# Attention scores two groups ahead in the main loop of a fused attention and two-layer expert kernel

## The chip, the cores and the metric

The kernel runs on one NeuronCore of a Trainium2 chip. The metric is the device time in microseconds (us) of one execution, as the median of several runs. Beside it stands one profiled execution with its trace, from which all durations here are read. TensorE does the matmuls and the transposes of 128x128 blocks, VectorE (DVE) and ScalarE (ACT) the elementwise work, GpSimd (POOL) a few small operations and the indirect transfers, SyncE (SP) issues most transfers.

## The reference

Three parts follow each other. Attention works inside chunks of 64 positions, for 8 batches and 8 heads of width 64; a feed-forward layer squares the relu; the last part sends each of 4608 tokens to one of 8 experts. Everything is float32.

```python
# attention, per chunk of 64 of the 576 positions (9 chunks a batch)
scores = scale * np.matmul(q_c, k_c.transpose(0, 1, 2, 4, 3))
scores = scores - np.max(scores, axis=-1, keepdims=True)
attn = np.exp(scores)
attn = attn / (np.sum(attn, axis=-1, keepdims=True) + 1e-09)
out = np.matmul(attn, v_c)
# x: (4608, 512)
h = np.maximum(x @ w_in, 0.0)          # (4608, 2048)
x = (h * h @ w_out)                    # (4608, 512)
# routing: normalised x against 8 normalised expert vectors, argmax, softmax weight
# per expert e: out[mask] = gate_w[mask, None] * (np.maximum(x[mask] @ w1[e], 0.0) @ w2[e])
```

## The kernel before

The 4608 tokens are cut into 18 groups of 256 (`TG`); a group holds four chunks of 64 positions. Groups 0 and 1 run in an opening part with its own planner. The main loop, `for n in range(2, NG)`, runs groups 2 to 17, one after the other, in the order in which the code is written: each engine takes its instructions in that order, and waits for what an instruction needs.

In one pass `n` of the loop TensorE does the feed-forward layer of group n. The **first product** (`l1`, line 389) runs over 16 tiles m: 12 matmuls each into a tile `l` of PSUM. ScalarE applies relu, square and a copy to the high half of `g` (`relu`, `square`, `ghi`), VectorE makes the low half (`glo`, line 408). The **second product** (`l2`, line 413) is done for two halves of 128 tokens (tt = 0, 1), each in four pieces u = 0 to 3 of 12 matmuls. The tiles `l` of both products share a ring `mm` of four PSUM banks. The results of the second product go through the router (`route`), whose steps stand in a list `todo`; `pop` takes one per tile m from m = 2 on, and three per piece of the second product. So the copy that empties the last bank of the second product (`a0`) comes only with m = 4 of the next pass. The router has eight products with the expert vectors (line 440), a tail of small VectorE operations (lines 460 to 467), an exponential on ScalarE (line 470), and a counting step with two small matmuls (lines 476, 477) and a transfer of the rows to `x2d`.

Between these stands the attention of the next group, n+1, in steps of one function each:

- `load_qk2`: transfers of q and k on SP's queue, into two buffers of the pool `stg`. There are 16 transfers each for q and k, or 32 each where the group's four chunks lie in two batches; group 4 (chunks 16 to 19, boundary at 18) is such a group. A buffer comes free with the transpose that reads it.
- `p1t`: one VectorE transpose for q, one for k (line 208), with m = 14 and m = 15 of the first product.
- `p2p`: the scores on TensorE (line 219), in 64x64 blocks, at piece 1 of the second product.
- `p2v`, `p2e`, `p2b`: maximum and subtraction (VectorE, lines 229, 231), exponential (ScalarE, line 234), sum, reciprocal and multiplication (VectorE, lines 239 to 242).
- `p3`: turns on TensorE (line 248) and a copy by ScalarE, at piece 4.
- `p4`: the values on TensorE (line 260), again in 64x64 blocks, at piece 5, then the high half by ScalarE and the low half by VectorE (lines 268, 269) into `xT`, which the next first product reads. There is one `xT`.

The pieces are counted through both halves, so piece 4 is the first one of the half tt = 1.

Of the kernel before, what the change touches and what calls it, by code (L numbers as in the profile page):

```python
# [7 lines left out]
F32 = mybir.dt.float32  # L8
# [4 lines left out]
AF = mybir.ActivationFunctionType  # L13
ALU = mybir.AluOpType
AX = mybir.AxisListType
# [5 lines left out]
def tile_attention_moe_moe2(  # L21
# [14 lines left out]
    V, S, G, PE = nc.vector, nc.scalar, nc.gpsimd, nc.tensor  # L36
# [4 lines left out]
    TG = 256  # L41
    KD = DM // 128
    KF = DFF // 128
# [31 lines left out]
    def f32(ap):  # L75
        return ap.bitcast(F32)
# [13 lines left out]
    duo = {}  # L90
# [72 lines left out]
    raws, at = {}, {}  # L163
# [26 lines left out]
    def load_qk2(n):  # L190
        c0 = 4 * n
        for nm, src in (("q", q), ("k", k)):
            t = stg_p.tile([128, 4, 8, 32], F32, tag="stg", name=nm)
            raws[nm, n, "w"] = t
            for h in range(4):
                for g in range(4):
                    c = 0
                    while c < 4:
                        b, r = divmod(c0 + c, CPB)
                        m = min(4 - c, CPB - r)  # L200
                        nc.sync.dma_start(
                            out=t[32 * g:32 * g + 32, h, 2 * c:2 * (c + m)],
                            in_=src[b, 4 * (g // 2) + h, 64 * r:64 * (r + m), 32 * (g % 2):32 * (g % 2) + 32].rearrange("(t i) x -> i t x", i=32))
                        c += m

    def p1t(n, nm):
        o = duo["t"].tile([128, 4, TG], F32, tag="tt", name=nm + "T")
        V.transpose(out=o.rearrange("p h (t i) -> p h t i", t=8), in_=raws.pop((nm, n, "w")))
        at[nm + "2"] = o

    def p2p(n):
        qT, kT = at.pop("q2"), at.pop("k2")
        sc = at["sc2"] = at_p.tile([128, 2, 512], F32, tag="at", name="sc")
        for u in range(2):
            for h in range(4):
                for c in range(2):
                    for j in range(2):
                        t0 = 128 * u + 64 * c
                        PE.matmul(
                            out=sc[64 * c:64 * c + 64, j, u * 256 + h * 64:u * 256 + (h + 1) * 64],  # L220
                            lhsT=qT[64 * j:64 * j + 64, h, t0:t0 + 64],
                            rhs=kT[64 * j:64 * j + 64, h, t0:t0 + 64],
                            start=True, stop=True,
                        )
# [9 lines left out]
        S.activation(out=at["ss"], in_=at["ss"], func=AF.Exp, scale=0.125)  # L234

    def p2b():
        s = at["ss"]
        sm = duo["m"].tile([128, 8, 2, 1], F32, tag="sm2", name="smm")
        V.tensor_reduce(out=sm, in_=s, op=ALU.add, axis=AX.X)
        V.tensor_scalar_add(out=sm, in0=sm, scalar1=1e-9)  # L240
        V.reciprocal(out=sm, in_=sm)
        V.tensor_tensor(out=s, in0=s, in1=sm.to_broadcast([128, 8, 2, 64]), op=ALU.mult)

    def p3():
        s = at.pop("ss")
        ps = at_p.tile([128, 2, 512], F32, tag="at", name="s3")
        for g in range(8):
            PE.transpose(ps[:, g // 4, (g % 4) * 128:(g % 4 + 1) * 128], s[:, g].rearrange("p j k -> p (j k)"), ident)
        o = at["a2"] = duo["t"].tile([128, 4, TG], F32, tag="tt", name="aT")
        S.activation(out=o.rearrange("p (u a) b -> p u (a b)", u=2), in_=ps, func=AF.Copy)  # L250

    def p4(n, x):
        aT, vts = at.pop("a2").rearrange("p a (b t) -> p (a b) t", b=2), [raws.pop(("v", 2 * n + u)) for u in range(2)]
        ps = at_p.tile([128, 2, 512], F32, tag="at", name="s4")
        for u in range(2):
            for h in range(4):
                for c in range(2):
                    for j in range(2):
                        o = u * 256 + (h // 2) * 128 + 64 * c
                        PE.matmul(  # L260
                            out=ps[64 * (h % 2):64 * (h % 2) + 64, j, o:o + 64],
                            lhsT=vts[u][64 * j:64 * j + 64, c, h, :],
                            rhs=aT[64 * j:64 * j + 64, 4 * u + h, 64 * c:64 * c + 64],
                            start=True, stop=True,
                        )
        pv = ps.rearrange("p j (w y) -> p j w y", w=2)
        hi, lo = [y.rearrange("p w (j u) t -> p j w (u t)", j=2) for y in x]
        S.activation(out=hi, in_=pv, func=AF.Copy)
        V.tensor_tensor(out=lo, in0=pv, in1=f32(hi), op=ALU.subtract)
# [111 lines left out]
    x0 = xT[:, 0], xT[:, 1]  # L381
# [16 lines left out]
    def relu(ps):  # L398
        S.activation(out=ps, in_=ps, func=AF.Relu)  # L399

    def square(ps):
        S.activation(out=ps, in_=ps, func=AF.Square)  # L402

    def ghi(ps, g):
        S.activation(out=g[:, 0], in_=ps, func=AF.Copy)  # L405

    def glo(ps, g):
        V.tensor_tensor(out=g[:, 1], in0=ps, in1=f32(g[:, 0]), op=ALU.subtract)  # L408
# [217 lines left out]
    with tc.manual_schedule():  # L626
# [19 lines left out]
        for m in range(KF):  # L646
            if m < 14:
                sl = 9 + m // 2
                t = wb[:, m % 2, sl * DM:(sl + 1) * DM].rearrange("p (a t) -> p a t", a=2)
            else:  # L650
                t = gx_p.tile([128, 2, TG], F32R, name=f"gx{m}")
# [157 lines left out]
        p = 0  # L809
# [31 lines left out]
        for r in range(4):  # L841
            nc.sync.dma_start(
                out=x2d[NT - TG:NT, :].rearrange("(p r) (a c) -> p (r a) c", r=2, a=2)[:, r], in_=zr)
# [9 lines left out]
        for n in range(2, NG):  # L853
            last = n == NG - 1
            if last:
                attn.close()
                two = ctx.enter_context(tc.tile_pool(name="two", bufs=1, reuse_waits="tile"))
                XN, XE = (ctx.enter_context(tc.tile_pool(name=nm, bufs=2, reuse_waits="tile")) for nm in ("XN", "XE"))
                p2["X"] = XN, XE
                idx = p2["idx"] = two.tile([128, E, NCOL], I32, name="idx")  # L860
                pre = ExitStack()
                stx["p"] = pre.enter_context(tc.tile_pool(name="stx", bufs=2, reuse_waits="tile"))
            gs = []
            for m in range(KF):
                g = g_p.tile([128, 2, TG], F32R, tag="g", name="g")
                gs.append(g)
                if m == KF - 2 and n == 2:
                    solo.close()
                    duo["t"] = attn.enter_context(tc.tile_pool(name="tt", bufs=2))
                    duo["s"] = attn.enter_context(tc.tile_pool(name="s2", bufs=1))  # L870
                    duo["m"] = attn.enter_context(tc.tile_pool(name="m2", bufs=1))
                if m >= KF - 2 and not last:
                    p1t(n + 1, "qk"[m - KF + 2])
                ps = l1(m, x0)
                relu(ps)
                square(ps)
                ghi(ps, g)
                glo(ps, g)
                if m == 0 and not last:
                    load_qk2(n + 1)  # L880
                if m == 0 and last:
                    for _ in range(8):
                        e_load(stg_p, "stg")
                if last and m >= 6 and m % 2 == 0:
                    e_split(stg_p, "stg", G)
                if m >= 2:
                    pop(2 if last and m < 5 else 1)
            nxt = {}
            if not last:
                load_v(2 * n + 2)  # L890
                load_v(2 * n + 3)
                nxt = {1: [lambda: p2p(n + 1), p2v, p2e], 2: [p2b], 4: [p3], 5: [lambda: p4(n + 1, x0)]}
            for tt in range(2):
                ps = mm_p.tile([128, 512], F32, tag="mm", name="l2")
                for u in range(4):
                    for fn in nxt.get(4 * tt + u, []):
                        fn()
                    l2(gs, tt, 4 * u, 4 * u + 4, ps, wo, KF)
                    if last and tt == 1 and u == 2:
                        turn(early, xT, gx[0])  # L900
                    pop((3, 3, 3, 3, 2, 1, 1, 1)[4 * tt + u] if last else 3)
                    if last:
                        for _ in range((3, 3, 2, 2, 1, 0, 0, 0)[4 * tt + u]):
                            e_split(stg_p, "stg")
                r = route(2 * n + tt, ps, xt_x if last else None)
                if last and tt:
                    r.pop(0)()
                    todo.insert(0, r.pop(0))
                todo += r
# [166 lines left out]
```

## Time and profile before

| what | value |
|---|---|
| median of 3 runs | 1432.27 us (1432.26 to 1433.1) |
| the profiled execution | 1430.2 us, its span 1428.4 us |
| TensorE busy | 1367.7 us, 96% of the span |
| VectorE, ScalarE, GpSimd busy | 791.1, 644.3, 175.2 us |
| TensorE's granted clock, mean over the span | 0.982 of full speed |
| main loop in the span | from about 150 to about 950 us |

The span reaches from the first to the last instruction that the profiler saw; the time of the execution has a little more around it. A wait is told for an engine by what it waited for: "PE sc L219 <- DVE kT L208" is TensorE, which stood before the scores until VectorE's transpose of k was done. Matmuls are pipelined and their ends are modelled, so the time that one block takes is best read from the start of the block to the start of the next one. One `PE.matmul` on float32 blocks of 64x64 shows as two instructions in the trace: a block of 32 shows as 64.

### The profile page before, as it was taken

Reading aid. Unit: us, or ns where it says so; the run is one execution under the profiler, and the core shown is the slowest. Engines: PE = TensorE matmul, PEld = TensorE weight load, DVE = VectorE, ACT = ScalarE, POOL = GpSimd, SP = SyncE. Lnnn points to the kernel's source line nnn. Section 1 sums busy time; section 2 is a strip of 40 time slices with the busy share of each in tenths; the row PEclk is TensorE's granted clock in tenths of the full one; section 3 lists DMA queues with packets and bytes.
Section 4 is the critical chain, followed back from the end, with each engine's and each line's share of the span. In section 5 each row is a group of like instructions: output and inputs, shape, how many; then the busy total and the mean of one; then the engine's idle time right before and its main releaser. Section 6 shows DMA issues by size and latency. Waiting matters only on the chain. (4 is left out here: it accounts for less than half of the span.)

```text
span 1428.4 us, 27983 instructions
## 1 busy us (share of the span) xinstructions
PE 1367.7 (96%) x10780; PEld 1221.6 (86%) x10780; DVE 791.1 (55%) x2146; ACT 644.3 (45%) x1529; POOL 175.2 (12%) x189
## 2 busy tenths in 40 slices
PE   5699999999999999999999999998999999899998
PEld 4697889988998898899889988987889898788886
DVE  6878566657656675666576556754442222145424
ACT  4693535634553554355345535633442222145424
POOL 0000010000000100000100001323212121113110
PEclk6899999999999999999999999999999999999999
DMA  8533332122122212212212222136533111156412
GB/s 212 158 119 119 104 70 57 37 38 61 39 45 38 53 39 45 45 40 44 50 35 54 43 38 90 46 119 200 181 126 99 34 60 35 43 165 199 150 49 92
DMA packets 222794, 116.81 MB, mean 82 GB/s; under 512 B 191585, under 2 KB 192227, under 8 KB 222468
## 3 DMA queue, kind: packets, MB, share of 16 engines
q1 hardware_dynamic: 213508, 89.01, 23.9%
q0 software_dynamic: 9056, 25.35, 5.6%
q8 instruction: 99, 1.62, 0.5%
q14 instruction: 99, 0.81, 0.2%
q10 hardware_dynamic: 32, 0.02, 0.0%
HBM read 94.64 MB, written 20.19 MB: 80 GB/s over the span
## 5 line engine op out<-in xcount | busy, mean ns | idle before, releaser
L389 PE MATMUL l<-xT,wa 128*128 128x256 f32 x3168 | 382.6, 281 | 6.0 <-DVE wa L157 6.0
L389 PEld LDWEIGHTS l<-xT,wa 128*128 128x128 f32 x3168 | 378.1, 189 | 8.3 <-DVE wa L157 6.7
L413 PE MATMUL l<-wb,g 128*128 128x512 f32 x1536 | 373.2, 398 | 0.0
L413 PEld LDWEIGHTS l<-wb,g 128*128 128x128 f32 x1536 | 284.0, 188 | 65.7
L440 DVE CUSTOM_DVE_ANT_0 junk<-X,en 128x512 bf16<-128x512 f32 x240 | 166.3, 693 | 64.0 <-ACT X L433 60.8
L408 DVE TENSOR_TENSOR g<-l,g 128x256 fp32r<-128x256 f32 x264 | 110.3, 419 | 160.4 <-ACT g L405 157.1
L598 DVE SCALAR_TENSOR_TENSOR h<-m,h 128x256 fp32r<-128x256 f32 x144 | 60.9, 423 | 195.6 <-ACT h L597 189.0
L413 PE MATMUL m<-wa,h 128*128 128x512 f32 x576 | 139.3, 397 | 0.0
L399 ACT ACTIVATE l<-l 128x256 f32<-128x256 f32 x272 | 100.8, 371 | 68.6 <-PE l L389 60.7
L413 PEld LDWEIGHTS m<-wa,h 128*128 128x128 f32 x576 | 106.4, 188 | 24.2
L597 ACT ACTIVATE h<-m 128x256 fp32r<-128x256 f32 x144 | 55.1, 383 | 132.8 <-PE m L594 118.0
L405 ACT ACTIVATE g<-l 128x256 fp32r<-128x256 f32 x264 | 101.5, 384 | 8.5
L402 ACT ACTIVATE l<-l 128x256 f32<-128x256 f32 x272 | 100.1, 368 | 8.7
L490 POOL DMA_INDIRECT perm<-tid,pos x36 | 38.2, 1060 | 523.2 <-DVE pos L489 281.3
L594 PEld LDWEIGHTS m<-xc,wa 128*128 128x128 f32 x768 | 92.5, 189 | 0.6
L594 PE MATMUL m<-xc,wa 128*128 128x256 f32 x768 | 92.8, 281 | 0.0
L413 PE MATMUL m<-wb,h 128*128 128x512 f32 x336 | 81.9, 398 | 0.0
L609 POOL DMA_INDIRECT out_dram<-o,idx x38 | 38.5, 1014 | 326.9 <-ACT xc L79 140.1
L413 PEld LDWEIGHTS m<-wb,h 128*128 128x128 f32 x336 | 62.0, 188 | 14.1
L608 ACT ACTIVATE o<-m,gn 128x512 f32<-128x512 f32 x23 | 15.8, 688 | 114.6 <-PE m L413 71.2
L435 POOL TENSOR_TENSOR ss<-ss,half 128x1 f32<-128x1 f32 x36 | 28.1, 780 | 308.7 <-ACT l L434 165.2
L80 DVE TENSOR_TENSOR xc<-tp,xc 128x512 fp32r<-128x512 f32 x36 | 24.3, 684 | 69.1 <-ACT xc L79 69.1
(182 smaller groups left out, 1540.2 us busy)
## 6 DMA issues: line engine op xcount, KB each, us to landing
we<-in_moe_w_dram SPq DMA_DIRECT2D x124, 256.0 KB
v<-in_v_dram SPq DMA_DIRECT2D x144, 64.0 KB
x2d<-X SPq DMA_DIRECT2D x32, 258.0 KB
ws<-in_moe_w_in_dram SPq DMA_DIRECT2D x8, 1024.0 KB
ws<-in_moe_w_out_dram SPq DMA_DIRECT2D x8, 1024.0 KB
q<-in_q_dram SPq DMA_DIRECT2D x160, 32.0 KB
k<-in_k_dram SPq DMA_DIRECT2D x160, 32.0 KB
en<-embn SPq DMA_DIRECT2D x1, 2048.0 KB
```

What stands on the lines that cost most here:

```text
L389: PE.matmul(out=ps, lhsT=wi[:, a, m // 4, kt, (m % 4) * 128:(m % 4 + 1) * 128], rhs=x[b][:, :, kt, :], start=(n == 0), stop=(n == 3 * KD - 1),
L399: S.activation(out=ps, in_=ps, func=AF.Relu)
L402: S.activation(out=ps, in_=ps, func=AF.Square)
L405: S.activation(out=g[:, 0], in_=ps, func=AF.Copy)
L408: V.tensor_tensor(out=g[:, 1], in0=ps, in1=f32(g[:, 0]), op=ALU.subtract)
L413: PE.matmul(out=ps, lhsT=gs[kk][:, b, tt * 128:(tt + 1) * 128], rhs=wt[:, a, kk, :], start=(kk == 0 and n == 0), stop=(kk == last - 1 and ...
L440: V.tensor_tensor_reduce(out=junk.rearrange("p (g c) -> p g c", g=4), in0=rows(X)[:, :, 0:128], in1=en[:, e].rearrange("p (g c) -> p g c", ...
L490: G.indirect_dma_start(out=perm[:, :], out_offset=bass.IndirectOffsetOnAxis(ap=pos[:, 0:1], axis=0), in_=tid[:, i:i + 1], in_offset=None,)
L594: PE.matmul(out=ps, lhsT=v1[:, a, m // 4, kt, (m % 4) * 128:(m % 4 + 1) * 128], rhs=xt[:, b, :, kt, :], start=(n == 0), stop=(n == 3 * KD ...
L597: S.activation(out=g[:, 0], in_=ps, func=AF.Relu)
L598: V.scalar_tensor_tensor(out=g[:, 1], in0=ps, scalar=0.0, in1=f32(g[:, 0]), op0=ALU.max, op1=ALU.subtract)
L609: G.indirect_dma_start(out=out[:, :], out_offset=bass.IndirectOffsetOnAxis(ap=col, axis=0), in_=o, in_offset=None, bounds_check=NT - 1, oo ...
```

## The change

The scores are now made two groups ahead: in pass n those of group n+2 stand directly behind the values of group n+1 (piece 5), as one block. The softmax of these scores is spread: maximum, subtraction and exponential behind them, sum and reciprocal at m = 1 of the next pass, multiplication at m = 3 (`p2m`), turns at piece 1. The loads and the transposes of q and k are for group n+2 accordingly. The turned values go back into the buffer `s`, no longer into one of the pool `tt`. Pass 2 is the way in: it does the scores of group 3 at piece 0, and loads, transposes (pieces 2 and 3) and scores (piece 6) of group 4 too.

```diff
     def p2b():
-        s = at["ss"]
-        sm = duo["m"].tile([128, 8, 2, 1], F32, tag="sm2", name="smm")
-        V.tensor_reduce(out=sm, in_=s, op=ALU.add, axis=AX.X)
+        sm = at["sm2"] = duo["m"].tile([128, 8, 2, 1], F32, tag="sm2", name="smm")
+        V.tensor_reduce(out=sm, in_=at["ss"], op=ALU.add, axis=AX.X)
         V.tensor_scalar_add(out=sm, in0=sm, scalar1=1e-9)
         V.reciprocal(out=sm, in_=sm)
-        V.tensor_tensor(out=s, in0=s, in1=sm.to_broadcast([128, 8, 2, 64]), op=ALU.mult)
+
+    def p2m():
+        s = at["ss"]
+        V.tensor_tensor(out=s, in0=s, in1=at.pop("sm2").to_broadcast([128, 8, 2, 64]), op=ALU.mult)
...
-        o = at["a2"] = duo["t"].tile([128, 4, TG], F32, tag="tt", name="aT")
-        S.activation(out=o.rearrange("p (u a) b -> p u (a b)", u=2), in_=ps, func=AF.Copy)
-
-    def p4(n, x):
+        S.activation(out=s.rearrange("p (u a) j k -> p u (a j k)", u=2), in_=ps, func=AF.Copy)
+
+    def p4(n, x=None):
...
+        at["s4"] = ps
+        if x:
+            p4x(x)
+
+    def p4x(x):
+        pv = at.pop("s4").rearrange("p j (w y) -> p j w y", w=2)
...
-                if m >= KF - 2 and not last:
-                    p1t(n + 1, "qk"[m - KF + 2])
+                if m == 1 and n > 2 and not last:
+                    p2b()
+                if m == 3 and n > 2 and not last:
+                    p2m()
+                if m >= KF - 2 and n + 2 < NG or m >= KF - 2 and n == 2:
+                    p1t(n + 1 + (n > 2), "qk"[m - KF + 2])
...
-                if m == 0 and not last:
+                if m == 0 and n == 2:
                     load_qk2(n + 1)
+                if m == 0 and 2 < n < NG - 2:
+                    load_qk2(n + 2)
...
-                nxt = {1: [lambda: p2p(n + 1), p2v, p2e], 2: [p2b], 4: [p3], 5: [lambda: p4(n + 1, x0)]}
+                join = [lambda: p4(n + 1, x0)]
+                if n + 2 < NG:
+                    join = [lambda: p4(n + 1), lambda: p2p(n + 2), lambda: p4x(x0), p2v, p2e]
+                nxt = {1: [p3], 5: join}
+                if n == 2:
+                    load_qk2(n + 2)
+                    nxt = {0: [lambda: p2p(n + 1), p2v, p2e], 2: [p2b, p2m, lambda: p1t(n + 2, "q")], 3: [lambda: p1t(n + 2, "k")], 4: [p3], 6: join}
```

In what follows, `sc<-kT,qT` are scores, `s_...<-ident,s` turns, `s_...<-aT,v` or `s_...<-s,v` values, `l_...<-xT,wa` tiles of the first product, `l_...<-wb,g` matmuls of the second.

**TensorE, pass 2**, from the last tile of the first product to the first tile of pass 3, before:

```order
203 L389 MATMUL l_2134<-xT,wa 128x256 x12
204 L413 MATMUL l_2161<-wb,g 128x512 x12
205 L219 MATMUL sc<-kT,qT 64x64 x32
206 L413 MATMUL l_2161<-wb,g 128x512 x36
207 L248 MATMUL s_2254<-ident,s 128x128 x8
208 L413 MATMUL l_2253<-wb,g 128x512 x12
209 L260 MATMUL s_2285<-aT,v 64x64 x32
210 L413 MATMUL l_2253<-wb,g 128x512 x36
211 L389 MATMUL l_2378<-xT,wa 128x256 x12
```

and with the change:

```order
203 L395 MATMUL l_2134<-xT,wa 128x256 x12
204 L219 MATMUL sc<-kT,qT 64x64 x32
205 L419 MATMUL l_2227<-wb,g 128x512 x48
206 L250 MATMUL s_2324<-ident,s 128x128 x8
207 L419 MATMUL l_2323<-wb,g 128x512 x24
208 L261 MATMUL s_2369<-s,v 64x64 x32
209 L219 MATMUL sc<-kT,qT 64x64 x32
210 L419 MATMUL l_2323<-wb,g 128x512 x24
211 L395 MATMUL l_2485<-xT,wa 128x256 x12
```

The scores of group 3 (row 205 before, 204 now) have moved ahead of the whole second product, and those of group 4 (row 209 now) have come in behind the values, ahead of the last 24 matmuls.

**VectorE, pass 2**, behind the multiplication that ends the softmax of group 3 (`junk,lg` is a router product, two rows each; `xT<-` the low half of the values), before:

```order
264 L242 TENSOR_TENSOR s<-s,smm 128x1024
265 L440 ISA junk,lg<-X,en 128x512
...
269 L269 TENSOR_TENSOR xT<-s_2285,xT 128x2x2x256
```

and with the change:

```order
264 L244 TENSOR_TENSOR s<-s,smm 128x1024
265 L208 STREAM_TRANSPOSE qT<-q 128x1024
266 L208 STREAM_TRANSPOSE kT<-k 128x1024
267 L446 ISA junk,lg<-X,en 128x512
...
277 L275 TENSOR_TENSOR xT<-s_2369,xT 128x2x2x256
278 L229 TENSOR_REDUCE mx<-sc 128x16
279 L231 TENSOR_TENSOR s<-sc,mx 128x2x8x64
280 L446 ISA junk,lg<-X,en 128x512
```

The two transposes of group 4 now stand here, ahead of all eight router products (five of them in rows 267 to 276) and of the low half of the values, and the softmax of group 4 begins behind that.

**TensorE, a regular pass** (pass 3), from the first piece of the second product, before:

```order
231 L413 MATMUL l_2793<-wb,g 128x512 x12
...
235 L477 MATMUL pr<-oh,ones 128x8
236 L219 MATMUL sc<-kT,qT 64x64 x32
237 L413 MATMUL l_2793<-wb,g 128x512 x36
238 L248 MATMUL s_2905<-ident,s 128x128 x8
239 L413 MATMUL l_2904<-wb,g 128x512 x12
240 L260 MATMUL s_2936<-aT,v 64x64 x32
241 L413 MATMUL l_2904<-wb,g 128x512 x36
```

and with the change:

```order
231 L419 MATMUL l_2873<-wb,g 128x512 x12
...
235 L483 MATMUL pr<-oh,ones 128x8
236 L250 MATMUL s_2905<-ident,s 128x128 x8
237 L419 MATMUL l_2873<-wb,g 128x512 x36
238 L419 MATMUL l_2951<-wb,g 128x512 x12
239 L261 MATMUL s_2972<-s,v 64x64 x32
240 L219 MATMUL sc<-kT,qT 64x64 x32
241 L419 MATMUL l_2951<-wb,g 128x512 x36
```

The scores have left the place behind the first 12 matmuls, where the turns stand now, and follow the values without a full-array matmul between the two. On SP's queue the 64 transfers of group 4's q and k stand where they stood, directly behind the eight of v at the end of pass 2's first product; those of group 5 now follow them directly, ahead of a transfer to `x2d`, the loads of v and another transfer to `x2d`.

## Rows read from the trace of the kernel before

**Rows 1.** The page: busy time, share of the span and instructions of TensorE, and its granted clock in 40 equal slices of the span, in tenths of full speed (9 is 90% or more).

```profile
PE 1367.7 (96%) x10780; PEld 1221.6 (86%) x10780; DVE 791.1 (55%) x2146; ACT 644.3 (45%) x1529; POOL 175.2 (12%) x189
...
PEclk6899999999999999999999999999999999999999
```

**Rows 2.** The view of waits, TensorE, from 186 to 880 us: who waited for whom, us in total, times, longest.

```profile
PE sc L219 <- DVE kT L208: 6.2, 15, 1.0
```

**Rows 3.** The timeline of TensorE in a regular pass, 430 to 464 us: start, duration, engine, line, operation, out<-in, shape, count, and in brackets the idle time before it. Durations of TensorE hold a modelled end.

```profile
434.84 1.16 PE L219 MATMUL sc<-kT,qT 64*64 64x64 f32 x64 [0.36 <-DVE kT L208]
435.93 8.66 PE L413 MATMUL l<-wb,g 128*128 128x512 f32 x36
...
445.23 3.05 PE L413 MATMUL l<-wb,g 128*128 128x512 f32 x12
448.20 1.21 PE L260 MATMUL s<-aT,v 64*64 64x64 f32 x64
449.34 8.66 PE L413 MATMUL l<-wb,g 128*128 128x512 f32 x36
457.85 5.76 PE L389 MATMUL l<-xT,wa 128*128 128x256 f32 x48
...
463.52 0.72 PE L389 MATMUL l<-xT,wa 128*128 128x256 f32 x4
```

**Rows 4.** The timeline of TensorE in two short windows at the end of the scores' and of the values' block (435.7 to 436.0 and 449.1 to 449.4 us): the last 22 of the 64 instructions of each, so the start is that of the 43rd.

```profile
435.48 0.52 PE L219 MATMUL sc<-kT,qT 64*64 64x64 f32 x22
...
448.89 0.52 PE L260 MATMUL s<-aT,v 64*64 64x64 f32 x22
```

**Rows 5.** The timeline of VectorE in the same pass, 425 to 460 us.

```profile
433.56 1.22 DVE L208 STREAM_TRANSPOSE kT<-k 128x1024 f32<-128x1024 f32 x1
...
436.44 1.22 DVE L229 TENSOR_REDUCE mx<-sc 128x16 f32<-128x1024 f32 x1
437.69 1.22 DVE L231 TENSOR_TENSOR s<-sc,mx 128x1024 f32<-128x1024 f32 x1
440.04 1.22 DVE L239 TENSOR_REDUCE smm<-s 128x16 f32<-128x1024 f32 x1 [1.13 <-ACT s L234]
...
441.80 1.22 DVE L242 TENSOR_TENSOR s<-s,smm 128x1024 f32<-128x1024 f32 x1
...
450.52 1.22 DVE L269 TENSOR_TENSOR xT<-s,xT 128x1024 fp32r<-128x1024 f32 x1 [2.04 <-ACT xT L268]
451.66 0.68 DVE L440 CUSTOM_DVE_ANT_0 junk<-X,en 128x512 bf16<-128x512 f32 x1
...
455.94 0.15 DVE L460 TENSOR_SCALAR ss<-ss 128x1 f32<-128x1 f32 x1
...
457.39 0.22 DVE L467 TENSOR_SCALAR ex<-lg,m 128x8 f32<-128x8 f32 x1
```

**Rows 6.** The timelines of ScalarE and of VectorE, 457 to 475 us, at the start of the next pass: the router's exponential, the first relu (line 399) and the first low half of `g`.

```profile
457.65 0.21 ACT L470 ACTIVATE ex<-ex 128x8 f32<-128x8 f32 x1 [7.16 <-DVE ex L467]
457.76 0.18 ACT L470 ACTIVATION_READ_ACCUMULATOR ex<-ex 128x1 f32 x1
459.45 0.37 ACT L399 ACTIVATE l<-l 128x256 f32<-128x256 f32 x1 [1.50 <-PE l L389]
...
460.67 0.42 DVE L408 TENSOR_TENSOR g<-l,g 128x256 fp32r<-128x256 f32 x1 [3.05 <-ACT g L405]
```

**Rows 7.** The timeline of TensorE in pass 2, 183 to 215 us.

```profile
185.94 2.95 PE L413 MATMUL l<-wb,g 128*128 128x512 f32 x12
189.85 1.16 PE L219 MATMUL sc<-kT,qT 64*64 64x64 f32 x64 [0.96 <-DVE kT L208]
190.95 8.66 PE L413 MATMUL l<-wb,g 128*128 128x512 f32 x36
199.44 1.04 PE L248 MATMUL s<-ident,s 128*128 128x128 f32 x8
200.23 3.04 PE L413 MATMUL l<-wb,g 128*128 128x512 f32 x12
...
212.84 2.38 PE L389 MATMUL l<-xT,wa 128*128 128x256 f32 x19
```

**Rows 8.** The timeline of SP's queue, 185 to 245 us: the issuing of transfers, with the time that SP spent on them.

```profile
191.49 16.65 SPq L201 DMA_DIRECT2D q<-in_q_dram  x32
208.24 15.89 SPq L201 DMA_DIRECT2D k<-in_k_dram  x32
224.24 0.36 SPq L480 DMA_DIRECT2D x2d<-X  x1
```

**Rows 9.** The view by windows over the k half of that load: window, its length, busy time and count of TensorE, its weight loads, VectorE, ScalarE and GpSimd, then the granted clock, the mean busy share of the 16 DMA engines, and GB/s.

```profile
208.30:224.10 15.80, 15.80 (x119) 14.86 (x118) 7.66 (x35) 8.50 (x25) 1.60 (x2) 1.00 0.22 35
```

**Rows 10.** The timeline of VectorE in pass 2, 188 to 203 us: the transpose of k of group 3.

```profile
188.48 1.23 DVE L208 STREAM_TRANSPOSE kT<-k 128x1024 f32<-128x1024 f32 x1
```

**Rows 11.** TensorE beside its longest stand in the last part of the kernel: the timeline, 1240 to 1256 us, and two windows of 4 us behind that stand, with columns as in rows 9.

```profile
1246.06 10.18 PE L594 MATMUL m<-xT,wb 128*128 128x256 f32 x68 [5.25 <-issue]
...
1246.10:1250.10 4.00, 4.00 (x19) 4.00 (x20) 0.52 (x2) 0.90 (x2) 0.99 (x1) 0.50 0.04 10
1250.50:1254.50 4.00, 4.00 (x36) 4.00 (x35) 2.53 (x6) 2.33 (x6) 2.96 (x3) 1.00 0.74 218
```

**Rows 12.** The view of transfers, 223 to 227 us: what the DMA engines moved, in GB/s, in 40 slices of 0.1 us.

```profile
GB/s 54 12 0 54 76 35 3 5 74 71 17 0 12 69 72 12 0 31 76 50 25 334 392 372 351 413 330 351 83 0 0 13 36 46 102 143 138 72 126 159
```

More of the change, by code (lines that the diff above doesn't have):

```diff
@@ L236, in p2b @@
     def p2b():
-        s = at["ss"]
-        sm = duo["m"].tile([128, 8, 2, 1], F32, tag="sm2", name="smm")
-        V.tensor_reduce(out=sm, in_=s, op=ALU.add, axis=AX.X)
+        sm = at["sm2"] = duo["m"].tile([128, 8, 2, 1], F32, tag="sm2", name="smm")
+        V.tensor_reduce(out=sm, in_=at["ss"], op=ALU.add, axis=AX.X)
         V.tensor_scalar_add(out=sm, in0=sm, scalar1=1e-9)
         V.reciprocal(out=sm, in_=sm)
-        V.tensor_tensor(out=s, in0=s, in1=sm.to_broadcast([128, 8, 2, 64]), op=ALU.mult)
+    def p2m():
+        s = at["ss"]
+        V.tensor_tensor(out=s, in0=s, in1=at.pop("sm2").to_broadcast([128, 8, 2, 64]), op=ALU.mult)
     def p3():
-        s = at.pop("ss")
+        s = at["ss"]
         ps = at_p.tile([128, 2, 512], F32, tag="at", name="s3")
@@ L248, in p3 @@
             PE.transpose(ps[:, g // 4, (g % 4) * 128:(g % 4 + 1) * 128], s[:, g].rearrange("p j k -> p (j k)"), ident)
-        o = at["a2"] = duo["t"].tile([128, 4, TG], F32, tag="tt", name="aT")
-        S.activation(out=o.rearrange("p (u a) b -> p u (a b)", u=2), in_=ps, func=AF.Copy)
-    def p4(n, x):
-        aT, vts = at.pop("a2").rearrange("p a (b t) -> p (a b) t", b=2), [raws.pop(("v", 2 * n + u)) for u in range(2)]
+        S.activation(out=s.rearrange("p (u a) j k -> p u (a j k)", u=2), in_=ps, func=AF.Copy)
+    def p4(n, x=None):
+        aT, vts = at.pop("ss").rearrange("p g j k -> p g (j k)"), [raws.pop(("v", 2 * n + u)) for u in range(2)]
         ps = at_p.tile([128, 2, 512], F32, tag="at", name="s4")
@@ L265, in p4 @@
                         )
-        pv = ps.rearrange("p j (w y) -> p j w y", w=2)
+        at["s4"] = ps
[3 more added lines that the diff above has]
+        pv = at.pop("s4").rearrange("p j (w y) -> p j w y", w=2)
         hi, lo = [y.rearrange("p w (j u) t -> p j w (u t)", j=2) for y in x]
```

## The prediction

> **What bounds the kernel now.** I read the page first: TensorE is busy for 96% of the span and its clock is at the full level from the third slice of forty on [rows 1]. So time is won only where TensorE stands still, and lost wherever it is made to. The view of waits for the stretch with the single-group loop (groups 2 to 16 prepare attention) has one entry for TensorE: the scores wait for `kT`, 6.2 us in 15 times [rows 2]. The longest, 0.96 us, is in group 2 [rows 7]; the other fourteen are 5.24 us together, 0.374 us each. In a regular group the reader sees why [rows 3, 5]: `kT` starts on VectorE at 433.56, ends at 434.78, and the scores start at 434.84, one piece of the second product after the first product's end.
>
> The rows show a second, smaller loss, at each change between the full array and the 64x64 blocks. A run of 36 matmuls of the second product takes 8.51 us up to the next start, 0.236 each [rows 3]; the 12 ahead of the values take 448.20 - 445.23 = 2.97 instead of 2.84: 0.13 to enter. Inside the blocks the step is (448.89 - 448.20)/42 = 16.4 ns for the values and (435.48 - 434.84)/42 = 15.2 for the scores [rows 4], so 64 of them are 1.05 and 0.98; the starts behind them come 1.14 and 1.09 after the block's: about 0.10 to leave. A round trip costs 0.23.
>
> **The regular groups.** Scores for group n+2 stand behind the values of n+1. Their `qT`, `kT` come at the same place of the first product as before, now some 14 us ahead of use, so the wait goes. The values leave the array in 64x64 shape, which I take as a seam of no cost: that round trip goes as well (bounds: 0 or 0.23 saved). In groups 3 to 15 each saves 0.374 + 0.23 = 0.60, thirteen times 7.85. Group 16 has no scores left: 0.374 + 0.13 + 1.09 = 1.6. Together 9.4 us.
>
> The moved work needs cover. ScalarE does the same count of operations; the turned values go back into `s`, so no `tt` buffer is needed. VectorE gets maximum and subtraction (2.5 us, from 436.44 to 438.9) behind the low half of the values, and sum with reciprocal (1.76, 440.04 to 441.80) and multiplication (1.22) inside the first product [rows 5]. From a start S of the values: the low half runs from S+2.32 to 3.54; maximum and subtraction to 6.05; six router products of 4.28 (451.66 to 455.94) to 10.33; the router's tail of 1.67 (to 457.61) to 12.0 [rows 5]. The first product starts at S + 1.05 + 0.98 + 0.10 + 8.51 = 10.64, and its first relu is 1.60 later, 12.24 [rows 3, 6]; the router's exponential ahead of it on ScalarE ends 0.33 behind the tail, 12.33. So the relu is 0.1 late. The low half of its tile starts 1.22 after the relu and takes 0.42 [rows 6]: 13.97. Sum and reciprocal reach 15.73, the next low half 16.15. Until the fifth tile the second product's last tile still holds one of the four banks, so tile m+3 takes the bank of tile m, and the fifth tile, due at 10.64 + 5.67 = 16.31, needs that second low half. It fits by 0.16. Regular groups have cover, though little.
>
> **Group 2, where the two-ahead order starts.** Here lies the largest term. Before, SP issues the loads of q and k of group 4 from 191.49 to 224.13: 64 transfers, 32.6 us, 0.51 each [rows 8]; nothing needs them until the end of group 3's first product. In the new order SP has them at the same place, behind the values' loads, and their buffers come free at the same transposes as before, so they are issued at the same times. But now both transposes of group 4 stand on VectorE in the second product of group 2, and the scores of group 4 stand on TensorE ahead of its last 24 matmuls. The last packets of k land at about 225.1: after that the view of transfers jumps to over 330 GB/s, the packets of the X row block that SP issues next [rows 12]. I take `kT` from 225.2 to 226.4 and the scores from 226.5.
>
> When does TensorE arrive? Its first product ends at 185.94. It then waits for `kT` of group 3, ready at 189.71, until 189.85, as before, but without the 12 matmuls (2.84) that ran under that wait [rows 7, 10]. Scores to 190.95; 48 matmuls, 11.33, to 202.3; turns 0.79; 24 matmuls and the entry, 5.80, to 208.9; values 1.05 to 209.9. It stands for 16.6 us. Then scores, leaving and 24 matmuls, 6.75: the next first product could start at 233.25 instead of 212.84, a loss of 20.4.
>
> VectorE waits in `kT` too, and everything behind that instruction is late: five router products (3.6), the low half of the values (1.25), maximum and subtraction (2.5), three router products (2.15), the tail (1.67). That is 11.2 us from 226.4, 237.6. ScalarE's relu follows at 237.9, the low half ends 1.22 + 0.42 later at 239.55, and the fourth tile can start at 239.6. Sum and reciprocal reach 241.3, the second low half 241.75, the fifth tile starts at 241.8. Before it would be 212.84 + 5.67 = 218.5. Loss 23.3.
>
> The clock comes on top or under this. Where TensorE stood for 5.25 us near the end, the granted clock showed the lower level (1.2 GHz), and for 4 us after work came back: 19 matmuls in 4.0 us at 0.50 against 36 at 1.00 [rows 11]. That is 4.0 x (1 - 19/36) = 1.9 us. With it the first three tiles end about 239.3, before the fourth may start at 239.6: hidden under VectorE's late chain. I add nothing.
>
> **Sum.** +23.3 - 9.4 = +13.9. The profiled execution, 1430.2 us (span 1428.4), becomes 1444.1; the median of the runs is 2.1 above the profiled one, so 1446.1 us.
>
> Bounds. Low: all 64 issues at the k half's 0.497 (15.89/32) land 0.8 earlier, and neither backlog nor lower clock shows: 20.4 - 0.8 - 9.4 = +10.2, 1442.5. High: backlog and clock added, 25.2; no round trips saved, 6.4: +18.8, 1451.1.
>
> **Rivals.**
> A: regular groups lose their cover. If the second low half comes over 0.16 us late in each group, TensorE waits for a bank in thirteen groups. Price: 0.3 more is 3.9 us, all of the saving 7.85: 1450 to 1454. For it: the margin is 0.16 on a chain of twelve durations. Against: before, VectorE idles 3.05 us ahead of that first low half [rows 6], and the moved work is counted into all of it. Chance 0.12.
>
> B, the other side: faster, because the loads land in time. SP's issue, not the data, paces them: over the k half the 16 DMA engines are 22% busy and move 35 GB/s [rows 9]. Were the data the limit, 32.6 x 0.22 is 7 us, landing near 200, `kT` near 202.5, and TensorE arrives at 209.9 without a stall. Group 2 would then cost 209.9 + 6.75 - 212.84 = 3.8, the change would give 3.8 - 9.4 = -5.6: 1426.7 us. It decides where the stall is below 5.6 us: loads landed by 214, 0.35 us an issue instead of 0.51. Against it: the same 64 transfers, from the same start, in this very trace. Chance 0.06.
> The Trainium skill (DMA: Bandwidth & Descriptors, section "Issuing engines are not separate DMA queues") says that the time in which a sequencer initiates a DMA is usually small beside the DMA itself. By that rule B would hold and the sum be its 1426.7; the trace disagrees, 32.6 us of issue against some 7 us of engine work, and the measurement decides.
>
> C: the stall comes but is shorter (another overlap, the loads started sooner): 1429 to 1441. Nothing in the trace gives it; 0.04.
>
> **How the numbers follow.** The likeliest case, the stall with regular savings, has 0.78 and gives 1446.1, with its own range 1442.5 to 1451.1. The range for all, 1441 to 1452, takes in half of A and leaves out B, C and the rest of A, some 0.16. A measurement of this kernel can tell about 0.2%, 2.9 us: faster is B, 0.06; same takes part of C, 0.03; slower 0.91.
>
> **What would show it.** Right: one wait of TensorE for `kT`, about 16.6 us, near 210 us, and one of some 3.9 near 186; no other wait for `kT`; a granted clock below 1.00 near 225 to 231; the values and scores as one block of 128 instructions from group 3 on, with 0.6 us less from one block to the next; group 3's first product about 22 us late. Wrong: `kT` of group 4 long done when TensorE gets to its scores, or waits for the tiles `l` in each regular group.

## The result and the profile after

The kernel with the change takes 1442.44 us (median of 4 runs, 1440.46 to 1444.56) against 1432.26 before (4 runs, 1431.85 to 1433.1): a ratio of 1.0071, 95% interval 1.0053 to 1.0088. It is slower, by 10.2 us, and the interval leaves out 1. The profiled execution took 1440.46 us, its span 1438.3, so 9.9 more than the span before.

The page after, lines as in [rows 1]:

```profile
PE 1367.1 (95%) x10780; PEld 1222.3 (85%) x10780; DVE 785.1 (55%) x2146; ACT 645.6 (45%) x1529; POOL 174.0 (12%) x189
...
PEclk6899997999999999999999999999999999999999
```

TensorE has the same number of instructions and, within 0.6 us, the same busy time as before. What is new is one slice, the seventh (215.7 to 251.7 us), in which the granted clock is below nine tenths. The view of waits, TensorE, 150 to 960 us, which answers to [rows 2]:

```profile
PE sc L219 <- DVE kT L208: 18.7, 2, 15.0
```

Fifteen short waits for `kT` became two long ones, both in pass 2. TensorE there, columns as in [rows 7]:

```profile
188.45 1.29 PE L219 MATMUL sc<-kT,qT 64*64 64x64 f32 x64 [3.75 <-DVE kT L208]
189.67 12.85 PE L419 MATMUL l<-wb,g 128*128 128x512 f32 x48
202.36 1.03 PE L250 MATMUL s<-ident,s 128*128 128x128 f32 x8
203.15 5.84 PE L419 MATMUL l<-wb,g 128*128 128x512 f32 x24
208.91 1.21 PE L261 MATMUL s<-s,v 64*64 64x64 f32 x64
225.12 1.99 PE L219 MATMUL sc<-kT,qT 64*64 64x64 f32 x64 [15.00 <-DVE kT L208]
227.04 7.32 PE L419 MATMUL l<-wb,g 128*128 128x512 f32 x24
234.20 5.76 PE L395 MATMUL l<-xT,wa 128*128 128x256 f32 x48
239.86 3.41 PE L395 MATMUL l<-xT,wa 128*128 128x256 f32 x27
```

Pass 3 begins at 234.20 instead of 212.84. Two stands are seen, and behind each of them blocks that are longer than usual: 48 matmuls from 189.67 to 202.36 (12.69 us; 48 of them in a regular pass take 11.38, from 453.28 to 464.66 below), scores of 1.92 us from 225.12 to 227.04 instead of 1.09, and 24 matmuls of 7.16 from 227.04 to 234.20, where the same 24 took 5.76 from 203.15 to 208.91. What the second stand waits for is on SP's queue, columns as in [rows 8], and on VectorE:

```profile
190.09 15.78 SPq L201 DMA_DIRECT2D q<-in_q_dram  x32
205.97 16.45 SPq L201 DMA_DIRECT2D k<-in_k_dram  x32
```

```profile
207.18 1.25 DVE L208 STREAM_TRANSPOSE qT<-q 128x1024 f32<-128x1024 f32 x1 [10.81 <-DMA q<-in_q_dram]
223.73 1.25 DVE L208 STREAM_TRANSPOSE kT<-k 128x1024 f32<-128x1024 f32 x1 [15.30 <-DMA k<-in_k_dram]
...
239.12 0.36 DVE L414 TENSOR_TENSOR g<-l,g 128x256 fp32r<-128x256 f32 x1
```

SP issues the 64 transfers of q and k from 190.09 to 222.42 (205.97 + 16.45), back to back, 0.505 us each. VectorE stands in each of the two transposes until its half has landed. The windows of TensorE's clock, columns as in [rows 9]:

```profile
189.30:192.70 3.40, 3.40 (x30) 2.70 (x20) 2.45 (x2) 0.40 (x1) 0.00 (x0) 0.51 0.35 73
...
225.10:230.30 5.20, 5.18 (x72) 4.41 (x73) 5.06 (x12) 0.00 (x0) 0.00 (x0) 0.50 0.37 59
230.30:235.00 4.70, 4.70 (x25) 3.94 (x24) 4.46 (x14) 1.06 (x1) 0.00 (x0) 1.00 0.40 65
```

The lower level (1.2 GHz) shows behind both stands (the times in which TensorE waits): behind the one of 3.75 us until 192.7, behind the one of 15.00 us until 230.3.

A regular pass after, beside [rows 3]; the last row is where pass 16 starts, for the mean over the passes:

```profile
427.02 5.76 PE L395 MATMUL l<-xT,wa 128*128 128x256 f32 x48
...
449.58 2.96 PE L419 MATMUL l<-wb,g 128*128 128x512 f32 x12
...
453.28 11.45 PE L419 MATMUL l<-wb,g 128*128 128x512 f32 x48
464.66 1.15 PE L261 MATMUL s<-s,v 64*64 64x64 f32 x62
...
465.70 1.10 PE L219 MATMUL sc<-kT,qT 64*64 64x64 f32 x62
466.73 8.66 PE L419 MATMUL l<-wb,g 128*128 128x512 f32 x36
475.23 0.98 PE L395 MATMUL l<-xT,wa 128*128 128x256 f32 x7
...
860.88 1.33 PE L395 MATMUL l<-xT,wa 128*128 128x256 f32 x10
```

and from the trace before, to compare with:

```profile
261.77 5.76 PE L389 MATMUL l<-xT,wa 128*128 128x256 f32 x48
...
284.34 2.03 PE L413 MATMUL l<-wb,g 128*128 128x512 f32 x8
...
408.75 5.76 PE L389 MATMUL l<-xT,wa 128*128 128x256 f32 x48
...
431.47 2.96 PE L413 MATMUL l<-wb,g 128*128 128x512 f32 x12
...
849.81 1.45 PE L389 MATMUL l<-xT,wa 128*128 128x256 f32 x11
```

Values and scores are one block (464.66 to 466.73, 2.07 us for 128 instructions; the last values and the first scores alternate). Thirteen passes, 3 to 15, take 860.88 - 234.20 = 626.68, 48.21 each; before, 849.81 - 212.84 [rows 7] = 636.97, 49.00 each. So the change does save in every regular pass what it was costed for, and more, and loses it all, and 10 us beside, in pass 2.

### The profile page after: what moved, and what is told of

Read it like the earlier page. It is cut to its first block, busy times and chain, and to the rows that moved or that the text cites. A ratio compares the mean times of both kernels' runs of the same rounds, so it can differ in the third digit from the quotient of the medians.

```text
span 1438.3 us, 28001 instructions
## 1 busy us (share of the span) xinstructions
PE 1367.1 (95%) x10780; PEld 1222.3 (85%) x10780; DVE 785.1 (55%) x2146; ACT 645.6 (45%) x1529; POOL 174.0 (12%) x189
## 5 line engine op out<-in xcount | busy, mean ns | idle before, releaser
L439 ACT ACTIVATE X<-l 128x512 f32<-128x512 f32 x32 | 19.1, 595 | 103.4 <-PE l L419 88.6
```

## The experiments

The theory: the loss is the load of group 4, 64 issues on one queue, which the way in of pass 2 needs some 15 us before they have landed; the regular passes gain. The rivals: pass 2 costs this whatever group it loads; the data, not the issue, is late; the gain in the regular passes is the wait alone.

**The way in one pass later.** In the kernel with the change, pass 2 works as before, and pass 3 is the way in; its pass needs group 5, with 32 transfers instead of 64, in place of group 4.

```diff
...
-                if m >= KF - 2 and n + 2 < NG or m >= KF - 2 and n == 2:
-                    p1t(n + 1 + (n > 2), "qk"[m - KF + 2])
+                if m >= KF - 2 and n + 2 < NG:
+                    p1t(n + 1 + (n > 3), "qk"[m - KF + 2])
...
-                if m == 0 and n == 2:
+                if m == 0 and n <= 3:
                     load_qk2(n + 1)
-                if m == 0 and 2 < n < NG - 2:
+                if m == 0 and 3 < n < NG - 2:
                     load_qk2(n + 2)
...
                 if n == 2:
+                    nxt = {1: [lambda: p2p(n + 1), p2v, p2e], 2: [p2b, p2m], 4: [p3], 5: [lambda: p4(n + 1, x0)]}
+                if n == 3:
                     load_qk2(n + 2)
```

> The changed kernel with the two-ahead order begun one pass later: pass 2 as in the kernel before, pass 3 is the way in and loads group 5 (16 transfers each for q and k instead of 32). Theory (the stall is SP's issue of group 4's 64 transfers, and it is the whole loss): kT of group 5 is ready near 256 us, before TensorE arrives near 259, so no long wait; pass 3 costs about 3.8 us more than before, twelve regular passes give 0.79 each and pass 16 gives 1.8: about 1425 us. Rival (the way in stalls wherever it stands, because both transposes lie ahead of the router on VectorE): a wait of 10 us or more in pass 3, about 1436 to 1442 us.

It took 1426.51 us (1424.07 to 1428.6), ratio to before 0.9955 (0.9938 to 0.9972). The long wait is gone. One stand is left, the first one of the way in, ahead of the scores at piece 0; pass 3 here:

```profile
211.59 5.76 PE L395 MATMUL l<-xT,wa 128*128 128x256 f32 x48
...
237.63 1.99 PE L219 MATMUL sc<-kT,qT 64*64 64x64 f32 x64 [3.33 <-DVE kT L208]
239.55 5.02 PE L419 MATMUL l<-wb,g 128*128 128x512 f32 x12
244.41 0.18 PE L482 MATMUL pr<-oh,tri 128*128 128x8 bf16 x1
...
267.27 5.76 PE L395 MATMUL l<-xT,wa 128*128 128x256 f32 x48
```

The way in by itself does not cost the 22.8 us; with the 64 transfers of group 4 it does. One term was expected too small: the way-in pass took 55.68 us (211.59 to 267.27), 6.75 over the 48.93 of the same pass before, where 3.8 were expected. The scores there stand 3.33 us, the clock is at the lower level from 237.0 to 243.8, and scores and 12 matmuls take 1.92 and 4.86 (239.55 to 244.41) instead of 1.09 and 2.80: 2.9 us that a stand of 3.33 costs beside itself.

**Half the issues.** The kernel with the change, but group 4 reads the q and k of group 5, whose chunks lie in one batch: the same bytes in 32 transfers instead of 64.

```diff
-        c0 = 4 * n
+        c0 = 4 * (5 if n == 4 else n)
```

> The changed kernel, except that group 4 takes q and k from the addresses of group 5: the same bytes in the same runs of 128 B, but 16 transfers each instead of 32 (so the q and k of group 4 are another group's, and its part of the output is changed). Theory (the number of transfers that SP issues sets the time): the load takes 16.6 us instead of 32.6, kT of group 4 is ready near 209, the wait of 15.0 us falls under 1 us, no lower clock, about 1424 us. Rival (bytes or packets set it): the load still ends near 223, the wait stays at 15 us, 1442 us.

1426.11 us (1424.8 to 1428.13), ratio 0.9953 (0.9937 to 0.997). SP's queue, VectorE, and TensorE's waits for `kT`:

```profile
190.96 8.31 SPq L201 DMA_DIRECT2D q<-in_q_dram  x16
199.37 7.79 SPq L201 DMA_DIRECT2D k<-in_k_dram  x16
```

```profile
208.76 1.25 DVE L208 STREAM_TRANSPOSE kT<-k 128x1024 f32<-128x1024 f32 x1 [6.85 <-DMA q<-in_q_dram]
```

```profile
PE sc L219 <- DVE kT L208: 3.8, 1, 3.8
```

An issue takes 0.52 and 0.49 us, though it carries twice the bytes. Half the issues end at 207.16, the transpose is done at 210.0, before TensorE has ended the values (211.5), and the 15-us stand is gone, with everything else in place: here a transfer of half the size cost the queue as much as a whole one, and the number of issues decided. The 3.8 left is the first stand, ahead of group 3's scores, with its lower clock (187.5 to 194.3), which the expectation of 1424 did not count.

**The issues shared by two engines.** The kernel with the change, the 32 transfers of k of group 4 on GpSimd.

```diff
-                        nc.sync.dma_start(
+                        (G if n == 4 and nm == "k" else nc.sync).dma_start(
```

> The changed kernel with the 32 transfers of k of group 4 issued on GpSimd's queue instead of SP's, beside those of q. Theory (issue time on one sequencer is what is short): q lands near 207; if GpSimd issues one in 0.5 us k lands there too and the wait falls under 1 us, about 1424 us; if it takes about 1 us for each, as its indirect transfers do (1.06 us), k lands near 223 and the wait stays, about 1442 us. Rival (the DMA engines are short): with both at once each is slower, the wait stays near 15 us although GpSimd has issued all by 207.

1428.67 us (1426.91 to 1431.37, 9 runs), ratio 0.9976 (0.9966 to 0.9986). GpSimd, VectorE and TensorE:

```profile
189.91 16.42 POOL L201 DMA_DIRECT2D k<-in_k_dram  x29 [2.16 <-DVE g L414]
206.76 1.71 POOL L201 DMA_DIRECT2D k<-in_k_dram  x3 [0.43 <-issue]
```

```profile
211.53 1.25 DVE L208 STREAM_TRANSPOSE kT<-k 128x1024 f32<-128x1024 f32 x1 [1.85 <-DMA k<-in_k_dram]
```

```profile
212.92 1.16 PE L219 MATMUL sc<-kT,qT 64*64 64x64 f32 x64 [1.87 <-DVE kT L208]
...
225.42 1.67 PE L395 MATMUL l<-xT,wa 128*128 128x256 f32 x12 [1.34 <-DVE g L414]
```

The same 64 transfers, issued side by side, moved 69 GB/s from 191.0 to 207.6 instead of 35, and the stand fell from 15.00 to 1.87 us. So the DMA engines had room, and one sequencer's issuing was short. The second row of TensorE is the wait for the low half of a tile, VectorE's late chain, that I had put into pass 2: it shows here, 1.34 us, where TensorE itself was less late. The time is 4.7 us over the 1424 that was expected for an issue of 0.5 us: one took 0.57 on GpSimd, k was used only at 211.53, and the first stand is here too, 3.71 us, with the lower level behind it.

**The transposes alone.** The kernel before, with the two transposes two tiles earlier from pass 3 on, and nothing else.

```diff
-                if m >= KF - 2 and not last:
-                    p1t(n + 1, "qk"[m - KF + 2])
+                lead = 2 if n == 2 else 4
+                if KF - lead <= m < KF - lead + 2 and not last:
+                    p1t(n + 1, "qk"[m - KF + lead])
```

> The kernel before, with the transposes of q and k two tiles earlier (m = 12 and 13 instead of 14 and 15) from pass 3 on. Scores stay where they were. Theory (the wait for kT is 0.374 us in each of 14 passes, and the rest of the saving of 0.79 a pass belongs to the change between full array and 64x64 blocks): the 14 waits go, 5.2 us, about 1427 us, passes of about 48.6 us. Rival (the wait is most of the saving): passes fall to about 48.2 us, about 1421 us.

1424.62 us (1424.07 to 1425.7), ratio 0.9948 (0.9932 to 0.9965). The waits and a regular pass:

```profile
PE sc L219 <- DVE kT L208: 1.0, 1, 1.0
```

```profile
477.07 2.96 PE L413 MATMUL l<-wb,g 128*128 128x512 f32 x12
...
480.01 1.16 PE L219 MATMUL sc<-kT,qT 64*64 64x64 f32 x64
...
503.00 1.22 PE L389 MATMUL l<-xT,wa 128*128 128x256 f32 x9
```

This splits the gain of a regular pass. From the first 12 matmuls of the second product to the next first product it is 26.38 us before (431.47, above, to 457.85 [rows 3]), 25.93 here (477.07 to 503.00), 25.65 with the change (449.58 to 475.23). The wait was worth 0.45, the round trip 0.28.

**Both, and the way in later.** The first of these experiments, with the transposes two tiles earlier in every pass behind pass 2, and in pass 3 the scores of group 4 back at piece 1 and the transpose of k at piece 5.

```diff
-                if m >= KF - 2 and n + 2 < NG:
-                    p1t(n + 1 + (n > 3), "qk"[m - KF + 2])
+                lead = 2 if n == 2 else 4
+                if KF - lead <= m < KF - lead + 2 and n + 2 < NG:
+                    p1t(n + 1 + (n > 3), "qk"[m - KF + lead])
...
                 if n == 3:
                     load_qk2(n + 2)
-                    nxt = {0: [lambda: p2p(n + 1), p2v, p2e], 2: [p2b, p2m, lambda: p1t(n + 2, "q")], 3: [lambda: p1t(n + 2, "k")], 4: [p3], 6: join}
+                    nxt = {1: [lambda: p2p(n + 1), p2v, p2e], 2: [p2b, p2m, lambda: p1t(n + 2, "q")], 4: [p3], 5: [lambda: p1t(n + 2, "k")], 6: join}
```

> Way in at pass 3 as in the run that began one pass later, but scores of group 4 at piece 1 and their transposes two tiles earlier, and the transpose of k of group 5 behind two router products (piece 5). Theory (the 6.7 us that pass 3 cost more there are 3.3 us of standing, 2.9 us of the lower clock behind it and the scores' block): no stand, no lower clock, pass 3 of about 49.7 us, regular passes 48.21: about 1420 to 1421 us, 3 to 4 us under the kernel with only the earlier transposes. Rival (the way in costs 5 us or more by its order alone): pass 3 of 54 us or more, about 1425 us.

1422.29 us (1419.38 to 1425.4), ratio 0.9929 (0.9915 to 0.9943). Pass 3 took 49.57, as expected, the regular passes 48.21. Pass 4 took 52.16, which was not: the other group with 64 transfers, group 6, is loaded there (issued from 250.45 to 282.97), and the earlier transposes ask for it before it can be used:

```profile
286.36 1.25 DVE L208 STREAM_TRANSPOSE kT<-k 128x1024 f32<-128x1024 f32 x1 [3.07 <-issue]
```

```profile
289.43 0.18 PE L482 MATMUL pr<-oh,tri 128*128 128x8 bf16 x1 [2.04 <-DVE oh L472]
```

VectorE stands 3.07 us in `kT`, the counting step behind it is late, and TensorE waits 2.04 us for that. The clock is at the lower level from 289.5 to 292.9. From the last issue of k to the transpose 3.39 us passed here (282.97 to 286.36), where it was 1.31 in the changed kernel (222.42 to 223.73).

**The scores away from the values.** As the last, but in the passes from 4 on the scores stand one piece (12 matmuls) behind the values, so that each has a round trip of its own.

```diff
+                if n > 3 and n + 2 < NG:
+                    nxt = {1: [p3], 5: [lambda: p4(n + 1, x0)], 6: [lambda: p2p(n + 2), p2v, p2e]}
```

> The same kernel, except that in the regular passes the scores stand at piece 6, 12 matmuls of the second product behind the values, so that the array changes to 64x64 blocks and back twice again; no wait for kT in either. Theory (one round trip costs 0.28 us of the pass): passes of 48.49 instead of 48.21 us, twelve of them 3.4 us: about 1424 us. Rival (blocks side by side save nothing, the gain is in the wait and in VectorE's order): passes stay at 48.21 us, same time as the kernel with both.

1427.02 us (1422.45 to 1430.21, 7 runs), ratio 0.9963 (0.9949 to 0.9978), 4.7 us over the kernel with both, and the intervals do not meet. A regular pass:

```profile
479.38 2.96 PE L419 MATMUL l<-wb,g 128*128 128x512 f32 x12
...
494.46 1.21 PE L261 MATMUL s<-s,v 64*64 64x64 f32 x64
495.60 3.06 PE L419 MATMUL l<-wb,g 128*128 128x512 f32 x12
498.58 1.16 PE L219 MATMUL sc<-kT,qT 64*64 64x64 f32 x64
...
505.38 5.76 PE L395 MATMUL l<-xT,wa 128*128 128x256 f32 x48
```

From 479.38 to 505.38 are 26.00 us against 25.65: the second round trip costs 0.35. The pass is longer by 0.51, not 0.28 as expected; the remaining 0.16 lies in the first product, which takes 22.71 us here (456.67 to 479.38) and 22.56 with the change (427.02 to 449.58).

Up to the end of pass 4's first product this kernel is the one with both, and its SP issued the transfers of group 6 within 0.3 us of the same times (250.14 to 282.80). Yet the transpose of k stood for 0.92 us only:

```profile
284.24 1.25 DVE L208 STREAM_TRANSPOSE kT<-k 128x1024 f32<-128x1024 f32 x1 [0.92 <-DMA k<-in_k_dram]
```

TensorE had no wait there, the clock stayed at the upper level, and pass 4 took 48.69. So the early place leaves the pass open to a late load, but the loss does not come in every execution.

**The transposes alone, again,** beside the last two on their chip.

> The kernel before with only the transposes two tiles earlier, run again beside the other two for a comparison on one chip: passes of 48.49 us, about 1424.6 us; the kernel with both is 3 to 4 us below it by the theory, level with it or above by the rival.

1423.33 us (1421.48 to 1425.78, 6 runs), ratio 0.9943 (0.993 to 0.9956), passes of 48.49 as the first time. The full two-ahead order (1422.29) is 1.0 us ahead of this one move, and the intervals overlap.

**Both, with the early transposes in pass 3 alone.**

```diff
-                lead = 2 if n == 2 else 4
+                lead = 4 if n == 3 else 2
```

> The kernel with both, with the early transposes in pass 3 alone; from pass 4 on they stand at m = 14 and 15 again, as in the changed kernel. Theory (the 52.16 us of pass 4 came from the transpose of k of group 6, whose 64 transfers SP ends only near 285, and from the lower clock behind that stand): pass 4 of 48.2 to 48.5 us, the rest as it was, some 3.7 us less: about 1418 to 1419 us. Rival (pass 4 pays for VectorE's late chain out of pass 3): pass 4 stays near 52 us, 1422 us.

1422.39 us (1419.61 to 1423.19), ratio 0.9935 (0.9921 to 0.9949). Pass 4 fell from 52.16 to 48.38, with no stand in the transposes: the later place avoids the loss, and VectorE's late chain out of pass 3 was not its cause. But with the early place too pass 4 took only 48.69 in the run above. What made k 2 us later in the one execution is open. The time of 1418 to 1419 that was expected was nearly met by the profiled execution (1419.61), not by the median. The profiled execution of the version before it was its longest run (1425.4): whether group 6 was late in its other runs is not known, and by their times the two versions can't be told apart.

## Why the prediction was right, and where its sizes were off

The forecast was 1446.1 us and slower; the median is 1442.44, inside the range of 1441 to 1452, near its lower end, and 0.06 below the likeliest case's own range (1442.5). The terms, span against span:

| stretch | predicted | measured | from |
|---|---|---|---|
| opening part | 0 | -1.41 | first product of pass 2 at 155.21, before 156.61 |
| pass 2 | +23.3 | +22.76 | 78.99 against 56.23 |
| passes 3 to 15 | -7.85 | -10.29 | 626.68 against 636.97 |
| pass 16 | -1.6 | -1.82 | 47.27 against 49.09 |
| pass 17 to the end | 0 | +0.65 | 530.15 against 529.50 |
| sum | +13.9 | +9.9 | |

The opening part and the part from pass 17 on are no work of the change: the code there is the same. The kernel with the transposes alone, whose code up to pass 3 is that of before, was 0.92 early there too, and the part from pass 17 on differed by up to 3.9 us between executions. Of the 4.0 us that the forecast is too high, 2.4 are the regular passes and 1.4 this opening.

**The stall of group 2: right.** The transfers stood where they were put, at 0.505 us an issue, and `kT` ended at 224.98; the 226.4 of the forecast, less the 1.41 of the opening, is 224.99. That it fits to 0.01 is luck: the issuing ended 0.3 sooner (222.42, where 224.13 less 1.41 is 222.72), and from there to the end of `kT` it took 0.3 longer (2.56 instead of 2.27). The two waits are those forecast, 3.75 (3.9) and 15.00 (16.6). That the long one is 1.6 shorter is no gain. The first stand already took the clock down: scores of 1.22 and 48 matmuls of 12.69 us instead of 1.09 and 11.33, so TensorE came 1.5 later to a place where it had to wait anyhow. I had not counted this; in pass 2 it is free, in the first and second experiment it is not.

**Which of the two chains is hidden: wrong way round, and by luck at no price.** I let VectorE's late chain (23.3) hide the lower clock (20.4 + 1.9). The clock cost 2.3: 9.08 from 225.12 to 234.20, instead of 6.75. VectorE was faster than I had it: the second low half ended at 239.48, where the forecast, less the opening, was 240.3. So TensorE reached its fifth tile at 239.86 with no wait for it: 20.4 + 2.3 = 22.7, measured as 22.76. The two chains happen to lie within 0.6 us of each other, so the term came out near 23.3 though the other one set it. That VectorE's chain stood close behind is shown by the shared issues, where it came out as a wait of 1.34 us.

**The regular passes: mechanism right, term too small.** The step that failed is "each saves 0.374 + 0.23 = 0.60"; it was 0.79. The wait was worth 0.45: the view of waits starts its count at the modelled end of the counting matmuls, and in the kernel without the wait the scores start before that end (at 480.01, where the last of them starts at 479.92 and takes 0.17). The round trip was worth 0.28 (transposes alone against the change) to 0.35 (scores apart): I took the step of the 36 matmuls behind a block, 0.236, as undisturbed, but 12 matmuls with no block ahead of them take 2.81, 0.234 each (449.58 to 452.39, where the counting step starts), so part of the price of leaving lay in what I compared with. The Trainium skill (TensorEngine Tiling (Array Packing), section "Key Properties") says that a change of the tiling mode, not of the tile alone, drains the engine. The 0.28 to 0.35 us agree with that; the page has no price. The rest, 0.06, is the first product: it takes 22.72 us in five of the thirteen passes before (408.75 to 431.47 in one) and 22.56 in the others (261.77 to 284.34), and 22.56 in all thirteen with the change.

**Rival A** (regular passes lose VectorE's cover) did not come. In the pass that starts at 475.23:

```profile
480.01 0.36 DVE L414 TENSOR_TENSOR g<-l,g 128x256 fp32r<-128x256 f32 x1
```

The second low half ends at 480.37, the fifth tile starts at 480.89: a margin of 0.52 where I had 0.16, and TensorE has no wait for `kT` or for a tile between 270 and 960 us.

**Rival B** (the loads land in time) did not come. It gave 1426.7 for that case, and where the issues were halved the kernel took 1426.11; this, too, is in part luck. Pass 2 cost 6.0 us there (62.20 against 56.23), not 3.8, for the lower clock behind the first stand, and the passes 3 to 16 gave 11.3 (674.78 against 686.06), not 9.4. The Trainium skill (DMA: Bandwidth & Descriptors, section "Issuing engines are not separate DMA queues") says that initiating on several engines saves only the time on the sequencer, which is usually small beside the DMA. Here it was not small: sharing the issues took 13.1 us from the stand. **Rival C** (a shorter stall, 1429 to 1441) did not come: the stall is the forecast one.

## What to carry to other kernels

Work that is moved ahead of its group moves its loads' deadline too: for the first pass of the new order, count the transfers by their number on the issuing queue too, not by their bytes alone, and if they are late, start the order one pass later. Where a wait of some tenths in every pass is the aim, first move its producer alone: two transposes two tiles earlier gave 7.5 to 8.1 us, and the whole two-ahead order, with its way in mended, some 9. A saving that is read from a wait's own length can be too small when that wait's start is a modelled end (0.37 here, where 0.45 was saved); the period of the loop, from start to start, is the measure.

## What the runs showed of the hardware that was not expected

- In pass 2 or 3 a stand of TensorE of 3.33 to 3.76 us was followed by the lower clock level in all four kernels that had one (the change, and the way in later, half the issues, the shared issues: 3.4 to 6.8 us at 0.5). One of 1.87 us (the shared issues) was not, one of 2.04 us in pass 4 of the kernel with both was (3.4 us at 0.5). In [rows 11] I had only one of 5.25. Behind the stand of 3.33 the work took 2.9 us more.
- 64x64 blocks of two different products, values and scores, follow each other without a seam: 128 instructions in 2.07 us, 16.2 ns each, as inside one block.
- Issuing on GpSimd cost 0.57 us a transfer (16.42 / 29), a little more than SP's 0.505, and the last of k was used only 3.1 us behind its last issue (208.47 to 211.53). On SP it was 1.3 in the changed kernel (222.42 to 223.73), but 3.4 in the kernel with both, so the difference is not shown to be the engine's.
- The first product runs in one of two steps, 22.56 or 22.72 us for the same 192 matmuls. In the regular passes it was mixed before (22.72 in five of passes 3 to 15), always the shorter with the change, and the longer from pass 5 on with the scores apart. The cause is open.
- The part of the program from pass 17 on differed by up to 3.9 us between profiled executions (529.2 to 533.1) with the same code there. So differences of 1 to 3 us between versions, which the passes show plainly, are not settled by their medians.
